# One decode step of attention: PE and DVE in a hand-made order, weights written over the scores, two accumulators, the last output weights behind all of V, two stores

## The chip, the cores and the metric

The kernel runs on one core of one Trainium2 chip. A core has a matrix engine (TensorE, PE in the profile, with its weight loads as PEld), a vector engine (VectorE, DVE), a scalar engine (ScalarE, ACT), GpSimd (POOL) and a queue engine (SyncE, SP), and 16 DMA engines that bring data from the chip's memory (HBM) into the core's own (SBUF). Matrix products land in PSUM, eight banks of 2 KB for each of 128 partitions, from where another engine takes them. The metric is device time in microseconds; before the change the median of three runs is 1333.25.

## What is computed

Everything is float32. Two requests (B = 2), one new token each, attend to a cache of 32768 positions; 32 query heads share 8 key and value heads, 4 to one. Beside it runs a small gated layer on the normalized token.

```python
B, Sq, D = 2, 1, 512
Hq, Hkv, Sk, Dh = 32, 8, 32768, 128

def _A_ref(x, k_cache, v_cache, wq, wo):
    q = (x @ wq).reshape(B, Sq, Hq, Dh).transpose(0, 2, 1, 3)
    k = jnp.repeat(k_cache, rep, axis=1)
    v = jnp.repeat(v_cache, rep, axis=1)
    scores = jnp.einsum("bhqd,bhkd->bhqk", q, k) * (Dh ** -0.5)
    p = _softmax(scores, axis=-1)
    o = jnp.einsum("bhqk,bhkd->bhqd", p, v)
    return o.transpose(0, 2, 1, 3).reshape(B, Sq, Hq * Dh) @ wo

def _B_ref(x, W_gate, W_up, W_down):          # D = 512, F = 1792
    gate = jnp.einsum("bsd,df->bsf", x, W_gate)
    up = jnp.einsum("bsd,df->bsf", x, W_up)
    h = gate * (gate > 0) * up
    return jnp.einsum("bsf,fd->bsd", h, W_down)

xn = _layernorm(x)
return x + _A_ref(xn, k_cache, v_cache, wq, wo) * _silu(_B_ref(xn, W_gate, W_up, W_down))
```

The two caches are 268 MB each and every byte is read once.

## The kernel before

**Tiles.** A group is one request and one key head: 32768 positions, in NU = 8 tiles of TK = 4096 positions, each 2 MB of K and 2 MB of V (16 KB in each of 128 partitions). There are NG = 16 groups and NK = 128 tiles of each kind; `group(g)` takes the two requests of a head one after the other.

**The ring.** All large loads, K, V and the weight matrices, share one pool of SLOTS = 8 slots of 16 KB per partition. All are issued on SP in `load` (line 123), in one order; a load waits on SP until the tile eight loads before it has been read for the last time. The loads run ahead of their use by DEPTH = 3 steps.

**A step.** The main loop (line 448) has one step for each K tile, and V follows K by OFF = 9 steps, since a group's maximum must be known before its weights are. In step `s`:

- `k_transposes(s)`: two VectorE transposes of 128x2048 (line 287) turn the K tile into the layout `kts` that the matrix engine needs.
- `scores(s)`: 16 matmuls (32 instructions in float32, line 298) with the query columns as weights, into a PSUM tile `s`; then VectorE scales them into an SBUF tile `sc` and keeps the running maximum (line 308).
- every eighth step `maximum(g)`: reduce over the group, transpose, reduce, broadcast back as a bias `nb`.
- `weights(v + 1)`: ScalarE takes exp (line 338), a matmul with a permutation spreads the result (`pt`, line 342), VectorE transposes it into one of three buffers `pts` (line 346).
- `values(v)`: 8 matmuls (16 instructions of 128x512, line 355) add weights times V into `o_ps`, one PSUM bank for all groups. The very last V tile is loaded and used in pieces, `LAST = (2, 1, 1)` quarters.
- at a group's end `sums` (the softmax's denominator), `take_o` (line 377: scale `o_ps` into `os`) and `finish_group` (line 386: gather the four query heads from the partitions into `ot`), and after the second request of a head the projection with the output weights `wo` (line 401), added to `yacc` or, for the last head, multiplied by the gate `gy` into `res` (lines 412 and 413).

The order in which PE and DVE issue this is not that of the text: the framework's planner orders the instructions of each engine by its own estimate of what is ready. The loads keep the order of the text. `ahead` holds what is loaded at which step, `extra` the matmuls of the small gated layer; `make_base` prepares `yacc * gy + x` shortly before the end. Output weights of head `hk` are loaded in the step that loads the last V tile of that head.

**The end.** The result lies in 4 x 2 rows of `res` and leaves in four stores, on POOL, SP, ACT and SP:

```python
for c, eng in enumerate((nc.gpsimd, nc.sync, nc.scalar, nc.sync)):
    eng.dma_start(out[:, 0, c * P : (c + 1) * P], res[32 * c : 32 * c + B, :])
```

Of the kernel before, what the change touches and what calls it, by code (L numbers as in the profile page):

```python
# [8 lines left out]
F32 = mybir.dt.float32  # L9
# [11 lines left out]
LAST = (2, 1, 1)  # L21
# [6 lines left out]
def kernel(  # L28
# [31 lines left out]
    spool = ctx.enter_context(tc.tile_pool(name="spool", bufs=NU + LAG + 3))  # L60
    work = ctx.enter_context(tc.tile_pool(name="work", bufs=2))
    ps_s = ctx.enter_context(tc.tile_pool(name="ps_s", bufs=3, space=PSUM))
# [48 lines left out]
    ot = const.tile([P, 2, 2, 32], F32, name="ot")  # L111
    nc.vector.memset(ot, 0.0)
# [5 lines left out]
    o_ps = ps_p.tile([P, NC, DH], F32, name="o_ps", bufs=1)  # L118
    nc.vector.memset(o_ps, 0.0)

    KT, VT, ST, PT, KTS, NBIAS, LS, MX, WO = {}, {}, {}, {}, {}, {}, {}, {}, {}
# [25 lines left out]
    def load_wo(hk):  # L147
        WO[hk] = ring.tile([P, 2, 2, D], F32, tag="r", align_bytes=ALIGN, name=f"wo_{hk}")
        r = REP * DH
        load(  # L150
            WO[hk].rearrange("p c i d -> p c (i d)"),
            wo[hk * r : (hk + 1) * r, :].rearrange("(c p i) d -> p c (i d)", c=2, i=2),
        )
# [78 lines left out]
    def mlp_gu(which):  # L232
        ps = ps_m.tile([P, 512], F32, tag="m", name=f"ps_{which}")
        for k in range(NKC):
            for c in range(4):
# [6 lines left out]
                )  # L242
        sb = work.tile([P, 512], F32, tag="row", name=f"sb_{which}")
        nc.vector.tensor_copy(sb[:, :FC], ps[:, :FC])
# [37 lines left out]
    def k_transposes(t):  # L282
        src = KT.pop(t).rearrange("p c j d -> p (c j d)")
        KTS[t] = ktpool.tile([P, NBLK * DH], F32, tag="kt", name=f"kts_{t}")
        half = NBLK * DH // 2
        for i in range(2):
            nc.vector.transpose(  # L287
                KTS[t][:, i * half : (i + 1) * half], src[:, i * half : (i + 1) * half]
            )

    def scores(t):
        g, u = divmod(t, NU)
        b, hk = group(g)
        ps = ps_s.tile([P, 256], F32, tag="s", name=f"s_{t}")
        mov = KTS.pop(t).rearrange("p (c j e k) -> p e c j k", c=NC, j=NJ, e=4)
        for e in range(4):
            for c in range(4):
# [6 lines left out]
                )  # L304
        if u == 0:
            MX[g] = work.tile([P, NU], F32, tag="mx", name=f"mx_{g}")
        ST[t] = spool.tile([P, 256], F32, tag="s", name=f"sc_{t}")
        nc.vector.tensor_scalar(  # L308
            ST[t], ps, SCALE, None, op0=ALU.mult, op1=ALU.max, accum_out=MX[g][:, u : u + 1]
        )  # L310

    def maximum(g):
        m = work.tile([P, 1], F32, tag="m", name=f"m_{g}")
        nc.vector.reduce_max(m, MX.pop(g), axis=AX.X)
        pr = ps_m.tile([P, 512], F32, tag="m", name=f"pr_{g}")
        nc.tensor.transpose(pr[:1, :P], m, ident)
# [14 lines left out]
        NBIAS[g] = work.tile([P, 1], F32, tag="nb", name=f"nb_{g}")  # L331
        nc.vector.tensor_copy(NBIAS[g], pr[:, 256:257])  # L332
        LS[g] = work.tile([P, NU], F32, tag="ls", name=f"ls_{g}")

    def weights(t):
        g, u = divmod(t, NU)
        st = ST.pop(t)
        nc.scalar.activation(  # L338
            st, st, AF.Exp, bias=NBIAS[g], scale=1.0, accum_out=LS[g][:, u : u + 1]
        )  # L340
        ps = ps_p.tile([P, 256], F32, tag="pt", name=f"pt_{t}")
        nc.tensor.matmul(  # L342
            ps, perm.rearrange("p k c h -> p (k c h)"), st, start=True, stop=True
        )
        PT[t] = work.tile([P, NJ, Q], F32, tag="pt", name=f"pts_{t}", bufs=3)
        nc.vector.transpose(PT[t].rearrange("p j m -> p (j m)"), ps)  # L346

    def values(t):
        g, u = divmod(t, NU)
        v, w = VT.pop(t), PT.pop(t)  # L350
        c = 0
        for n in (NC,) if t < NK - 1 else LAST:
            for j in range(NJ):
                a = Q * (j % 4)
                nc.tensor.matmul(  # L355
                    o_ps[a : a + n * REP, :n, :],
# [10 lines left out]
    def sums(g):  # L367
# [4 lines left out]
        RL[g] = work.tile([P, 1], F32, tag="rl", name=f"rl_{g}")  # L372
        nc.vector.reciprocal(RL[g], pr[:, :1])

    def take_o(g):
        OS[g] = work.tile([P, NC, DH], F32, tag="os", name=f"os_{g}")
        nc.vector.tensor_scalar(OS[g], o_ps, RL.pop(g), None, op0=ALU.mult)  # L377

    def finish_group(g):
        b, hk = group(g)  # L380
# [121 lines left out]
```

## Time and profile before

| | us |
|---|---|
| median of three runs | 1333.25 |
| lowest, highest | 1332.27, 1333.82 |
| the profiled execution | 1335.89 |
| its span | 1334.0 |
| PE busy | 881.1 |
| PE weight loads busy | 345.6 |
| DVE busy | 736.5 |
| ACT busy | 69.1 |
| HBM read | 564.67 MB |

The span is the time from the first to the last instruction in the profile; the profiled execution's own time has 1.89 us more around it. Busy times of different engines overlap. The strip over 40 slices gives the share of each engine in tenths and the rate of the DMA engines in GB/s. In the list of groups a line gives busy time, the mean of one instruction in ns, and the idle time before, with what ended it. In the timeline, a line gives start, length, engine, line of the kernel, operation, what is written from what, and in brackets the idle time before with what ended it. In a table of windows, the columns are the window, its length, the busy time of PE, PEld, DVE, ACT and POOL with their instructions, the granted clock of PE, the share of the DMA engines' time and GB/s.

### The profile page before, as it was taken

What the parts mean: (1) busy time and instruction counts of PE and PEld (TensorE: products, weight loads), DVE (VectorE), ACT (ScalarE), POOL (GpSimd) and SP (SyncE); (2) the same over time, 40 slices, a digit from 0 to 9 for tenths busy, and PEclk for the clock granted to TensorE, in tenths of its full rate; (3) what the DMA queues carried; (4) which work ended last, traced back from release to release, by engine and by line L of the source; (5) the groups of instructions that cost most, each with busy time, mean ns of one, the idle gap of its engine ahead of it and who ended that gap; (6) DMA issues with size and microseconds to landing.
All of it is one profiled execution on the core that took longest, in us unless ns stands there. A gap on an engine that the chain in (4) does not pass through costs nothing.

```text
span 1334.0 us, 17338 instructions
## 1 busy us (share of the span) xinstructions
PE 881.1 (66%) x7560; PEld 345.6 (26%) x7560; DVE 736.5 (55%) x976; ACT 69.1 (5%) x261; POOL 1.3 (0%) x7
## 2 busy tenths in 40 slices
PE   4767566766757666676666757667666766767657
PEld 1333222222213222232222312223222232213213
DVE  5765554555555555564555555465565555556462
ACT  0001010100101001010100101001010100101001
POOL 0000000000000000000000000000000000000000
PEclk9777887988878888788977888888887978878889
DMA  9999999999999999999999999999999999999996
GB/s 397 429 431 429 431 430 430 429 431 431 429 430 431 430 430 430 429 430 432 430 430 422 428 430 431 429 416 429 429 430 430 415 430 429 431 431 414 430 430 283
DMA packets 40907, 565.79 MB, mean 424 GB/s; under 512 B 4462, under 2 KB 4478, under 8 KB 6784
## 3 DMA queue, kind: packets, MB, share of 16 engines
q1 hardware_dynamic: 40776, 564.68, 99.4%
q8 instruction: 60, 0.98, 0.3%
q14 instruction: 15, 0.12, 0.0%
q10 hardware_dynamic: 24, 0.01, 0.0%
q0 software_dynamic: 32, 0.00, 0.0%
HBM read 564.67 MB, written 0.00 MB: 423 GB/s over the span
## 4 chain that ended last, share of the span: by engine, by line
issue 100%; POOLq 0%; POOL 0%
POOLq L497 0%; POOL ident masks.py:199 0%; POOL ident masks.py:197 0%; POOLq masks.py:199 0%; POOLq L484 0%
## 5 line engine op out<-in xcount | busy, mean ns | idle before, releaser
L298 PE MATMUL s<-kts,qt 128*32 128x256 f32 x4096 | 466.7, 522 | 388.9 <-DVE kts L287 373.7
L287 DVE STREAM_TRANSPOSE kts<-k 128x2048 f32<-128x2048 f32 x256 | 572.7, 2275 | 0.0
L355 PE MATMUL o_ps<-v,pts 128*16 128x512 f32 (+2 forms) x2080 | 360.2, 675 | 0.0
L298 PEld LDWEIGHTS s<-kts,qt 128*32 128x32 f32 x4096 | 180.2, 140 | 664.3 <-issue 351.6
L308 DVE TENSOR_SCALAR_CACHE_REDUCE sc<-s 128x256 f32<-128x256 f32 x128 | 54.3, 425 | 375.5 <-PE s L298 375.5
L346 DVE STREAM_TRANSPOSE pts<-pt 128x256 f32<-128x256 f32 x128 | 57.0, 448 | 137.9 <-PE o_ps L355 131.2
L355 PEld LDWEIGHTS o_ps<-v,pts 128*16 128x16 f32 (+2 forms) x2080 | 96.2, 116 | 141.6 <-issue 130.1
L338 ACT ACTIVATE sc<-sc,nb 128x256 f32<-128x256 f32 x128 | 63.2, 494 | 1147.3 <-DVE nb L332 1147.3
L342 PE MATMUL pt<-sc,perm 128*128 128x256 f32 x256 | 85.3, 439 | 33.4 <-DVE pts L346 32.2
L342 PEld LDWEIGHTS pt<-sc,perm 128*128 128x128 f32 x256 | 42.5, 198 | 99.7 <-issue 73.0
L386 PE MATMUL po<-sel,os 128*64 128x4 f32 x512 | 23.4, 204 | 3.9 <-DVE os L377 3.9
L386 PEld LDWEIGHTS po<-sel,os 128*64 128x64 f32 x512 | 22.0, 138 | 10.2 <-DVE os L377 10.2
L338 ACT ACTIVATION_READ_ACCUMULATOR sc<-sc,nb 128x1 f32 x128 | 23.9, 187 | 0.0
L377 DVE TENSOR_SCALAR os<-o_ps,rl 128x512 f32<-128x512 f32 x16 | 12.0, 750 | 17.3 <-PE o_ps L355 17.3
L401 PE MATMUL py<-wo,ot 128*32 128x128 f32 x256 | 19.2, 403 | 0.4 <-DVE ot L396 0.4
L396 DVE COPY ot<-po 64x4 f32<-64x4 f32 x32 | 5.2, 163 | 19.7 <-PE po L386 19.5
L401 PEld LDWEIGHTS py<-wo,ot 128*32 128x32 f32 x256 | 14.1, 153 | 2.5 <-issue 1.5
L192 PE MATMUL pq<-wq,xnt 128*32 128x512 f32 x64 | 10.1, 788 | 1.1 <-DMA wq<-in_A_wq_dram 0.8
L308 DVE DVE_READ_ACCUMULATOR sc<-s 128x1 f32 x128 | 10.7, 83 | 0.0
L180 PE MATMUL px<-ident,boot 32*128 32x32 f32 x4 | 0.9, 288 | 12.8 <-DVE boot L174 12.8
L214 DVE COPY qt<-pqt 32x16 f32<-32x16 f32 x64 | 8.6, 176 | 1.3 <-PE pqt L209 0.9
L332 DVE COPY nb<-pr 128x1 f32<-128x1 f32 x16 | 2.5, 159 | 12.2 <-PE pr L328 12.2
(70 smaller groups left out, 115.3 us busy)
## 6 DMA issues: line engine op xcount, KB each, us to landing
k<-in_A_k_cache_dram SPq DMA_DIRECT2D x128, 2048.0 KB, 18.7
v<-in_A_v_cache_dram SPq DMA_DIRECT2D x127, 2048.0 KB, 17.2
wq<-in_A_wq_dram SPq DMA_DIRECT2D x4, 2048.0 KB, 13.3
wo<-in_A_wo_dram SPq DMA_DIRECT2D x8, 1024.0 KB, 15.5
wg<-in_B_W_gate_dram SPq DMA_DIRECT2D x2, 1792.0 KB
wu<-in_B_W_up_dram SPq DMA_DIRECT2D x2, 1792.0 KB, 33.0
wd<-in_B_W_down_dram SPq DMA_DIRECT2D x2, 1792.0 KB
v<-in_A_v_cache_dram SPq DMA_DIRECT2D x1, 1024.0 KB
```

The lines of the kernel that those rows point to most:

```text
L192: nc.tensor.matmul(pq[half][32 * c : 32 * c + 32, :], xnt[:, k, :], wqt[k][:, half, c * 512 : (c + 1) * 512], start=(k == 0), stop=(k == N ...
L214: nc.vector.tensor_copy(qt[part, b, half * 4 : half * 4 + 4, :, kb * REP + h], src[:, :, :, b],)
L287: nc.vector.transpose(KTS[t][:, i * half : (i + 1) * half], src[:, i * half : (i + 1) * half])
L298: nc.tensor.matmul(ps[Q * c : Q * c + Q, :], qt[:, b, hk, e, :], mov[:, e, c], start=(e == 0), stop=(e == 3),)
L308: nc.vector.tensor_scalar(ST[t], ps, SCALE, None, op0=ALU.mult, op1=ALU.max, accum_out=MX[g][:, u : u + 1])
L338: nc.scalar.activation(st, st, AF.Exp, bias=NBIAS[g], scale=1.0, accum_out=LS[g][:, u : u + 1])
L342: nc.tensor.matmul(ps, perm.rearrange("p k c h -> p (k c h)"), st, start=True, stop=True)
L346: nc.vector.transpose(PT[t].rearrange("p j m -> p (j m)"), ps)
L355: nc.tensor.matmul(o_ps[a : a + n * REP, :n, :], w[:, j, c * REP : (c + n) * REP], v[:, c : c + n, j, :], start=(u == 0 and j < 4), stop=( ...
L377: nc.vector.tensor_scalar(OS[g], o_ps, RL.pop(g), None, op0=ALU.mult)
L386: nc.tensor.matmul(pr[64 * r : 64 * r + 64, i * REP : (i + 1) * REP], o2[:, c, i, :], sel[:, c, :], start=(c == 0), stop=(c == NC - 1),)
L401: nc.tensor.matmul(py[32 * c : 32 * c + 32, :P], ot[:, k // 2, k % 2, :], WO[hk][:, k // 2, k % 2, c * P : (c + 1) * P], start=(k == 0), s ...
```

## The change

**Order.** At the end of each step `pin()` chains the instructions that PE and DVE got in that step, in the order of the text, without a semaphore. The loop's text is rewritten for it: helpers are split into a matrix part and a take by VectorE. In step `s` VectorE has the first half of K's transposes, the taking of the scores of the step before, at a group's start the taking of the finished accumulator, the second half of the transposes, and the taking of the next weights. PE has the next weights, the gathering of a finished group, the scores, the projection, the sums and the values. The loop is one step longer.

**Weights over scores.** `take_weights` transposes the weights from PSUM back into the tile that held the scores (`ST`), and `values` reads them there; the pool has 13 such tiles instead of 12, and the three `pts` buffers go. All exps of a group are issued in `maximum`.

**Two accumulators.** `ops[g % 2]` takes the place of `o_ps`, `ots` holds two of what was `ot`; score tiles in PSUM are two instead of three.

**Output weights.** Those of the last two heads are loaded behind all of V, the last one in two halves; one projection adds both heads in PSUM. `LAST` is `(2, 2)`.

**Stores.** Two, one for each request, on SP and ACT.

```diff
-LAST = (2, 1, 1)
+LAST = (2, 2)
...
-    spool = ctx.enter_context(tc.tile_pool(name="spool", bufs=NU + LAG + 3))
+    spool = ctx.enter_context(tc.tile_pool(name="spool", bufs=NU + LAG + 4))
...
-    ps_s = ctx.enter_context(tc.tile_pool(name="ps_s", bufs=3, space=PSUM))
+    ps_s = ctx.enter_context(tc.tile_pool(name="ps_s", bufs=2, space=PSUM))
...
-    o_ps = ps_p.tile([P, NC, DH], F32, name="o_ps", bufs=1)
-    nc.vector.memset(o_ps, 0.0)
+    ops = [ps_p.tile([P, NC, DH], F32, name=f"o_ps_{i}", bufs=1) for i in range(2)]
+    for i in range(2):
+        nc.vector.memset(ops[i], 0.0)
...
+        if hk < HKV - 1:
+            load(dst, rows)
+        else:
+            for c in range(2):
+                load(dst[:, c], rows[:, c])
...
+    def take_weights(t):
+        nc.vector.transpose(ST[t].rearrange("p j m -> p (j m)"), PW.pop(t))
...
-        v, w = VT.pop(t), PT.pop(t)
+        v, w = VT.pop(t), ST.pop(t)
...
+    def project_o(hks):
+        py = ps_m.tile([P, 512], F32, tag="m", name=f"py_{hks[0]}")
+        for hk in hks:
+            w = WO.pop(hk)
...
     for hk in range(HKV):
-        at(ahead, (hk * B + B) * NU - 1 + OFF - DEPTH, load_wo, hk)
+        end = hk if hk < HKV - 2 else HKV - 1
+        at(ahead, (end * B + B) * NU - 1 + OFF - DEPTH, load_wo, hk)
...
+    def pin():
+        nonlocal pinned
+        for ins in block[pinned:]:
+            e = ins.engine
+            if e not in (mybir.EngineType.PE, mybir.EngineType.DVE):
+                continue
+            if e in last:
+                tc.add_manual_dep(
+                    ins,
+                    last[e].name,
+                    mybir.DependencyInfo(
+                        mybir.DependencyClass.NoSync, mybir.DependencyReason.DATA
+                    ),
+                    reason="order of issue",
+                )
+            last[e] = ins
+        pinned = len(block)
+
-    for s in range(NK + OFF):
+    for s in range(NK + OFF + 1):
         v = s - OFF
+        done = (v - 1) // NU if v > 0 and v % NU == 0 else None
+        live = 0 <= v + 1 < NK
+        first = (v + 1) // NU if live and (v + 1) % NU == 0 else None
         if s < NK:
-            k_transposes(s)
+            k_transpose(s, 0)
+        if 0 < s <= NK:
+            take_scores(s - 1)
+        if done is not None:
+            take_o(done)
+        for f, a in taken.get(s, []):
+            f(*a)
+        if first is not None:
+            tile_maximum(first)
+        elif live:
+            weights(v + 1)
+        if s < NK:
+            k_transpose(s, 1)
+        if first is not None:
+            maximum(first)
+        elif live:
+            take_weights(v + 1)
+        if done is not None:
+            finish_group(done)
+        if s < NK:
             scores(s)
...
+            if g % B == B - 1 and hk != HKV - 2:
+                project_o((hk,) if hk < HKV - 1 else (hk - 1, hk))
+        if first is not None:
             weights(v + 1)
+            take_weights(v + 1)
+        if 0 <= v < NK:
             if v % NU == NU - 1:
                 sums(v // NU)
             values(v)
...
+        pin()
...
-    for c, eng in enumerate((nc.gpsimd, nc.sync, nc.scalar, nc.sync)):
-        eng.dma_start(out[:, 0, c * P : (c + 1) * P], res[32 * c : 32 * c + B, :])
+    rows = res.rearrange("(c q) n -> q c n", q=32)
+    for b, eng in enumerate((nc.sync, nc.scalar)):
+        eng.dma_start(out[b, 0, :].rearrange("(c n) -> c n", c=4), rows[b])
```

138 lines of the change are left out of this document (76 added, 62 removed).

## The prediction

> **What bounds the kernel now.** I read the page's rates first, then the same rates cut into stages, then the waits of VectorE, the time from issue to landing of loads early and late, and last the timeline of the end.
>
> From the page:
>
> ```profile
> span 1334.0 us, 17338 instructions
> DVE  5765554555555555564555555465565555556462
> DMA  9999999999999999999999999999999999999996
> GB/s 397 429 431 429 431 430 430 429 431 431 429 430 431 430 430 430 429 430 432 430 430 422 428 430 431 429 416 429 429 430 430 415 430 429 431 431 414 430 430 283
> q1 hardware_dynamic: 40776, 564.68, 99.4%
> ```
>
> The loads run at 429 to 432 GB/s nearly throughout; VectorE (DVE) is busy about half of each slice. But four of the late slices dip to 414 to 422, and the last holds 283. The dips by stage (columns: window, length, busy of each engine, granted clock, DMA share, GB/s):
>
> ```profile
> 10.00:720.00 710.00, 469.30 (x3950) 184.26 (x3950) 399.85 (x555) 35.48 (x132) 0.00 (x0) 0.83 1.01 430
> 720.00:740.00 20.00, 13.04 (x130) 4.68 (x130) 12.55 (x11) 0.00 (x0) 0.00 (x0) 0.91 1.00 414
> ...
> 880.00:900.00 20.00, 12.61 (x130) 4.68 (x130) 12.75 (x10) 0.00 (x0) 0.00 (x0) 0.91 0.99 404
> ...
> 1040.00:1060.00 20.00, 12.18 (x127) 4.58 (x130) 13.18 (x10) 0.00 (x0) 0.00 (x0) 0.91 1.00 405
> ...
> 1200.00:1220.00 20.00, 11.76 (x120) 4.34 (x124) 13.61 (x10) 0.00 (x0) 0.00 (x0) 0.91 0.99 403
> ```
>
> Against 430 these four lose (16 + 26 + 25 + 27) x 20 / 430 = 4.4 us. Why there, and only late? Time from issue to landing, one line from each of four stages (issues at 240 to 320 us, at 1200 to 1280 us, the one K at 1209.3, and the kernel's very first load):
>
> ```profile
> k<-in_A_k_cache_dram SPq DMA_DIRECT2D x8, 2048.0 KB, 20.8
> ...
> k<-in_A_k_cache_dram SPq DMA_DIRECT2D x7, 2048.0 KB, 15.4
> ...
> k<-in_A_k_cache_dram SPq DMA_DIRECT2D x1, 2048.0 KB, 10.4
> ...
> wq<-in_A_wq_dram SPq DMA_DIRECT2D x1, 2048.0 KB, 7.7
> ```
>
> A load meets a backlog of 21 us early and of 15 us late: the queue is eaten up slowly, because slots of the ring come back a little more slowly than the loads could use them. At 1209.3 it is nearly empty (10.4, against 7.7 for a load that met nothing). So two chains run almost level: the loads, and the work that frees slots. That work's step:
>
> ```profile
> 1268.16 4.46 DVE L287 STREAM_TRANSPOSE kts<-k 128x2048 f32<-128x2048 f32 x2
> ...
> 1276.28 0.42 DVE L308 TENSOR_SCALAR_CACHE_REDUCE sc<-s 128x256 f32<-128x256 f32 x1 [3.65 <-PE s L298]
> ...
> 1278.00 0.45 DVE L346 STREAM_TRANSPOSE pts<-pt 128x256 f32<-128x256 f32 x1 [1.28 <-PE o_ps L355]
> ```
>
> 4.46 us of transposes, 3.65 waiting for the scores, 0.5 to take them, 1.28 waiting for the values, 0.45: 10.2 us with the seams. A K and a V tile are 4.19 MB, 9.75 us at 430 GB/s. Over the run:
>
> ```profile
> DVE sc L308 <- PE s L298: 375.5, 126, 3.7
> DVE pts L346 <- PE o_ps L355: 131.2, 79, 2.7
> ...
> DVE st L167 <- DMA boot<-in_A_x_dram: 2.9, 1, 2.9
> ```
>
> The end is the other place (timeline, then the landing of the load issued at 1310.17):
>
> ```profile
> 1310.17 0.38 SPq L123 DMA_DIRECT2D wo<-in_A_wo_dram  x1
> ...
> 1314.55 1.91 PE L355 MATMUL o_ps<-v,pts 128*16 128x512 f32 x16
> ...
> 1317.72 8.80 PE L355 MATMUL o_ps<-v,pts 128*16 128x512 f32 x112
> ...
> 1326.59 0.75 DVE L377 TENSOR_SCALAR os<-o_ps,rl 128x512 f32<-128x512 f32 x1 [4.72 <-PE o_ps L355]
> ...
> 1327.40 1.46 PE L386 MATMUL po<-sel,os 128*64 128x4 f32 x32 [0.87 <-DVE os L377]
> 1328.89 0.34 DVE L396 COPY ot<-po 64x4 f32<-64x4 f32 x2 [1.55 <-PE po L386]
> ...
> 1329.29 1.08 PE L401 MATMUL py<-wo,ot 128*32 128x128 f32 x32 [0.43 <-DVE ot L396]
> 1330.44 0.29 DVE L412 TENSOR_TENSOR res<-py,gy 128x128 f32<-128x128 f32 x1 [1.20 <-PE py L401]
> ...
> 1331.08 0.65 SPq L470 DMA_DIRECT2D out_dram<-res  x2
> ...
> 1331.35 0.65 POOL L470 DMA_DIRECT2D out_dram<-res  x1 [1330.04 <-DVE res L413]
> ```
>
> ```profile
> wo<-in_A_wo_dram SPq DMA_DIRECT2D x1, 1024.0 KB, 15.5
> ```
>
> The last load lands at 1310.17 + 15.5 = 1325.7; the last values end at 1326.5 and 7.5 us follow. How the loads end:
>
> ```profile
> 1322.00:1323.00 1.00, 1.00 (x16) 0.35 (x12) 0.00 (x0) 0.00 (x0) 0.00 (x0) 1.00 0.51 197
> ...
> 1324.00:1325.00 1.00, 1.00 (x16) 0.33 (x12) 0.00 (x0) 0.00 (x0) 0.00 (x0) 1.00 0.22 90
> ```
>
> Half the DMA engines have run out by 1322; the others work until about 1325. A tile has landed when its slowest engine is done, so the late half sets the end, and a pause of the early half in a dip costs nothing in itself.
>
> **The change, part by part. The hand-made order.** In a step VectorE now does: first half of the transposes, the previous tile's scores, second half, the next weights. The 3.65 us wait is covered by the weights and the next first half (0.45 + 2.2), the 1.28 goes because the transposed weights overwrite their own scores instead of waiting for one of three buffers. That leaves 4.46 + 0.5 + 0.45 = 5.4 us of VectorE in a step, against 9.75 of loads. What is late next is the landing of K: the transposes wait for it, and scores, weights and values are queued behind them. A V tile's slot then comes back some 13 us after it landed: 4.9 until its K is there, 5.4, and 2 to 4 for scores and values. V tiles reuse a slot four steps (39 us) on, so its next load still goes out about 25 us ahead: the queue does not run dry. TensorE (PE), should it run at half clock:
>
> ```profile
> 1282.88 3.20 PE L298 MATMUL s<-kts,qt 128*32 128x256 f32 x26 [1.48 <-DVE kts L287]
> ...
> 1291.40 1.70 PE L298 MATMUL s<-kts,qt 128*32 128x256 f32 x26 [1.48 <-DVE kts L287]
> ```
>
> The same 26 instructions take 1.88 times as long there: the 32 of the scores 3.9, the values (1.91 for a tile's 16, above) 3.6, the weights, two of the same width as the scores, 0.25 and their latency: about 8, still under 9.75.
>
> So the dips should go. What that is worth is bounded by 0 (all of them fell on the early engines) and by 4.4 us (all 16 alike). The K at 1209.3 took 10.4 us in the emptiest stretch against 7.7 without a backlog, so the late engines still had work there; the value is near the lower end. I take **-1.0**.
>
> **The end.** The output weights of head 6 (1.05 MB) go from 1199 to behind all of V, so two megabytes follow the last V instead of one. With the loads' end kept at 1325.7, V's last half lands 2.10 MB, 4.9 us, earlier: 1320.8. It needs 16 instructions of 128x256, 1.70 / 26 x 16 = 1.05: 1321.85. From the values' end (1317.72 + 8.80 = 1326.52) to the projection at 1329.29 are 2.77 us, unchanged: 1324.6. The projection now does two heads, 64 instructions, 2 x 1.08 = 2.16: 1326.8. It reaches the last half of the weights after 48 of them, at 1326.2, when that has landed. From its end (1330.37) to the store's issue at 1331.08: 0.71. From there the old end is 2.92 us away; the last of the four stores leaves POOL at 1332.0, the last of the two would leave SP about 1331.4, so 2.3. Sum: 1326.8 + 0.7 + 2.3 = 1329.8 against 1334.0: **-4.2**. That the compute arrives in time for this rests on the step above: TensorE has then nothing left over when V's last half lands, where now the last 112 instructions run without a pause from 1317.72.
>
> **At nothing:** clearing a second accumulator and a second ot, some tenths of a microsecond of VectorE ahead of the layernorm, where it waits 2.9 us for x (without that cover, nothing of it would reach the loads either, which have a backlog). The split of the last weights: one more issue of about 0.4 us on SP, which is waiting for slots. The softmax terms moved between queues, and the mlp's copies one step later: inside the 4 us per step that VectorE has free. Two score banks instead of three: the scores before last are long taken.
>
> **Against which time.** The profiled execution took 1335.89 (span 1334.0), 2.64 above the median 1333.25. Where those 2.64 sit no row shows. If in the compute at the end, which now lags V's landing, runs without a profile have that much less to win; bounds 0 and 2.6, and since the loads fill most of the span alike I take +0.8. Sum for the median: -4.2 - 1.0 + 0.8 = -4.4: **1328.9**, say 1329.
>
> **The rivals. Cold TensorE at the end.** Now TensorE waits for each V. The trace has this:
>
> ```profile
> 1279.43:1282.84 3.41, 0.62 (x4) 0.17 (x4) 3.40 (x2) 0.00 (x0) 0.00 (x0) 1.00 0.99 423
> 1282.84:1286.25 3.41, 3.37 (x30) 1.52 (x34) 0.00 (x0) 0.00 (x0) 0.00 (x0) 0.50 1.03 442
> ...
> 1296.49:1299.90 3.41, 1.93 (x33) 0.91 (x30) 1.73 (x1) 0.00 (x0) 0.00 (x0) 1.00 0.97 411
> ```
>
> A window of 3.41 us with 0.62 us of matmul is followed by one at half clock; one with 1.93 was not. At the end a V comes each 4.9 us with 1.91 + 0.25, about 2.2 us of matmul, so a window holds 0.8 to 2.2, and which it is depends on phase. Price if cold from V's last half on: values +0.9, po up to +1.3, projection +1.9, together 2 to 4, I take 3. Then -1.4: about 1332, no change. Against it: from V's next-to-last tile to the projection's end, 1.9 + 1.05 + 1.05 + 1.46 + 2.16 = 7.6 us of matmul fall into about 11.5 us (1315 to 1326.8), 2.2 per window. The Trainium skill ("TensorE: Matmul & The Clock Gate", Part 1: The HAM clock gate) says that TensorE falls to half rate after a whole idle window of about 3.4 us; the gaps of some 2.6 us here would by that leave it at full rate and the sum as it is. The rows above show it stricter: 0.62 us of work in a window did not save it, which is why this rival has a chance of 0.25.
>
> **All 16 engines lose in the dips.** Then the 4.4 us come back whole: -4.2 - 4.4 + 0.8 = -7.8, about 1325.4. For it: the share falls below 1.00. Against: 10.4 at 1209.3.
>
> **Slots come back later than now.** With VectorE's order fixed, everything of a step stands behind K's landing, and at a group's first step also behind the maximum, the scores and the first weights. Now a head of two groups takes 878.21 - 717.78 = 160.4 us, a group of 8 steps 80.2:
>
> ```profile
> 717.78 0.38 SPq L123 DMA_DIRECT2D wo<-in_A_wo_dram  x1
> ...
> 878.21 0.38 SPq L123 DMA_DIRECT2D wo<-in_A_wo_dram  x1
> ```
>
> If a group took longer than that, every microsecond over would cost 16, one per group: at 81, +13 us, 1346. My working gives 8 x 5.4 to 8 and, for that first step, an allowance of one more step: 49 to 72. It decides only above 80.2.
>
> **How the numbers follow.** The forecast has 0.50, all engines lose 0.13: faster, 0.63. The cold end, or a full 2.6 of the profile's surplus, 0.26: within 0.2% (2.7 us, about what a measurement of this kernel can tell from no change). Slots later: 0.11. The range goes from the second rival's end (1324.8) to the first's cold end with 4 us (1332.8); it leaves out the slow case and little more. The forecast's own: 1327 to 1330.5.
>
> **What the profile would show.** Right: no slice under 425 GB/s before the last; VectorE's wait for the scores down from 375 to under 60 us and idle time ahead of the transposes that ends with K's landing; times from issue to landing of 23 us or more also late; V's last half landed some 5 us before the last weights; TensorE at full clock in the last 10 us. Wrong: a dip that stays (something else than empty slots), a loads' end earlier than 1323 (the dips did cost all engines) or later than 1326, half clock after 1320, or a projection that waits for wo.

## The result

In the comparison of the two kernels on one chip the changed kernel takes 1330.95 us (median of 20 runs, 1330.04 to 1333.91), the kernel before 1333.67 (20 runs, 1332.27 to 1336.53). The ratio is 0.9981, 95% interval 0.9975 to 0.9987: a gain of 0.19%, about 2.5 us (the medians lie 2.7 apart), where the forecast had 4.4. It lies in the forecast's range, and just on the line of 0.2% between the case that was given 0.63 and the one that was given 0.26.

The profiled execution after the change takes 1330.78 us, its span is 1328.9: 5.1 us less than the profiled execution before, where the forecast had 5.2 ahead of its last term. So the two profiles agree with the sum, and the medians do not. The page after:

```profile
span 1328.9 us, 17052 instructions
DVE  5775555555645555554555555545555554646541
DMA  9999999999999999999999999999999999999996
GB/s 397 430 430 431 430 429 431 430 430 430 430 431 429 431 431 430 429 430 431 429 431 428 431 431 430 431 429 431 431 428 431 429 431 431 429 431 430 431 431 288
```

No slice but the first and the last is under 428 GB/s. Two of the stretches that dipped to 414 and 403, from a table of windows with the columns of before, and then VectorE's waits (us in total, times, longest) and the time from issue to landing of K tiles issued from 1200 to 1280 us:

```profile
720.00:740.00 20.00, 12.26 (x95) 4.75 (x99) 9.50 (x18) 4.04 (x16) 0.00 (x0) 0.74 1.00 426
...
1200.00:1220.00 20.00, 12.95 (x101) 5.11 (x101) 10.81 (x20) 4.04 (x16) 0.00 (x0) 0.83 1.01 431
```

```profile
DVE kts L298 <- DMA k<-in_A_k_cache_dram: 459.6, 114, 6.0
...
DVE sc L374 <- PE pt L365: 82.3, 22, 5.2
...
DVE sc L322 <- PE s L308: 5.5, 6, 1.7
```

```profile
k<-in_A_k_cache_dram SPq DMA_DIRECT2D x5, 2048.0 KB, 27.0
```

VectorE waited 375.5 us for scores and 131.2 for the values; now it waits 459.6 for K to land, and 82.3 for the spread weights, most of it in the first step of a group. A K load issued from 1200 to 1280 us lands 27.0 us later instead of 15.4. The end, in the timeline:

```profile
1314.88 3.37 PE L383 MATMUL o_ps<-v,sc 128*16 128x512 f32 x16 [1.03 <-DMA v<-in_A_v_cache_dram]
...
1318.49 2.20 PE L383 MATMUL o_ps<-v,sc 128*8 128x256 f32 x32
...
1319.64 0.55 PEld L383 LDWEIGHTS o_ps<-v,sc 128*8 128x8 f32 x16 [0.60 <-DMA v<-in_A_v_cache_dram]
1320.76 0.75 DVE L406 TENSOR_SCALAR os<-o_ps,rl 128x512 f32<-128x512 f32 x1 [1.99 <-PE o_ps L383]
...
1321.56 1.46 PE L416 MATMUL po<-sel,os 128*64 128x4 f32 x32 [0.87 <-DVE os L406]
...
1322.95 2.25 PE L434 MATMUL py<-wo,ots 128*32 128x128 f32 x64
...
1324.56 0.38 PEld L434 LDWEIGHTS py<-wo,ots 128*32 128x32 f32 x16 [0.35 <-DMA wo<-in_A_wo_dram]
...
1325.60 0.29 DVE L445 TENSOR_TENSOR res<-res,base 128x128 f32<-128x128 f32 x1
1325.91 0.65 SPq L551 DMA_DIRECT2D out_dram<-res  x1
1325.92 0.61 ACTq L551 DMA_DIRECT2D out_dram<-res  x1
```

V's last half has landed by 1319.6, the projection waits 0.35 us for the last half of the weights, which are there at 1324.6, and the stores leave at 1325.91, 5.2 us before those of the profiled execution before. From there to the end of the span it is 3.0 us, as before (2.92).

### The profile page after: what moved, and what is told of

Read it like the earlier page. It is cut to its first block, busy times and chain, and to the rows that moved or that the text cites. A ratio compares the mean times of both kernels' runs of the same rounds, so it can differ in the third digit from the quotient of the medians.

```text
span 1328.9 us, 17052 instructions
## 1 busy us (share of the span) xinstructions
PE 872.7 (66%) x7544; PEld 338.5 (25%) x7544; DVE 727.7 (55%) x976; ACT 69.1 (5%) x261; POOL 0.7 (0%) x6
## 4 chain that ended last, share of the span: by engine, by line
DMA 74%; DVE 14%; PE 11%; issue 0%; DVEq 0%
DMA k<-in_A_k_cache_dram 68%; DVE kts L298 12%; PE s L308 5%; PE o_ps L383 4%; DMA v<-in_A_v_cache_dram 2%; DMA wo<-in_A_wo_dram 2%; DMA wq<-in_A_wq_dram 2%; DVE sc L322 1%; PE pt L365 0%; DVE qt L220 0%; PE ps_u L242 0%; PE ps_d L281 0%; DVE os L406 0%; PE pq L198 0%; DVE boot L212 0%
## 5 line engine op out<-in xcount | busy, mean ns | idle before, releaser
L298 DVE STREAM_TRANSPOSE kts<-k 128x2048 f32<-128x2048 f32 x256 | 590.4, 2307 | 459.6 <-DMA k<-in_A_k_cache_dram 459.6
L308 PE MATMUL s<-kts,qt 128*32 128x256 f32 x4096 | 455.1, 526 | 326.5 <-DVE kts L298 322.5
L383 PE MATMUL o_ps<-v,sc 128*16 128x512 f32 (+1 forms) x2064 | 343.0, 685 | 6.2 <-DMA v<-in_A_v_cache_dram 6.1
L383 PEld LDWEIGHTS o_ps<-v,sc 128*16 128x16 f32 (+1 forms) x2064 | 91.4, 115 | 149.6 <-issue 136.4
L374 DVE STREAM_TRANSPOSE sc<-pt 128x256 f32<-128x256 f32 x128 | 53.1, 415 | 82.4 <-PE pt L365 82.3
L365 PE MATMUL pt<-sc,perm 128*128 128x256 f32 x256 | 94.5, 453 | 0.9 <-ACT sc L359 0.9
L351 PE MATMUL pr<-negone,mrow 1*128 1x1 f32 x32 | 8.9, 344 | 37.5 <-DVE mrow L348 37.5
L351 PEld LDWEIGHTS pr<-negone,mrow 1*128 1x128 f32 x32 | 7.5, 291 | 40.8 <-DVE mrow L348 40.8
L434 PE MATMUL py<-wo,ots 128*32 128x128 f32 x256 | 12.6, 313 | 0.1
L434 PEld LDWEIGHTS py<-wo,ots 128*32 128x32 f32 x256 | 10.5, 131 | 2.0 <-issue 0.9
```

What stands on the lines that cost most here:

```text
L298: nc.vector.transpose(KTS[t][:, i * half : (i + 1) * half], src[:, i * half : (i + 1) * half])
L308: nc.tensor.matmul(ps[Q * c : Q * c + Q, :], qt[:, b, hk, e, :], mov[:, e, c], start=(e == 0), stop=(e == 3),)
L351: nc.tensor.matmul(pr[:, 256:257], mrow.rearrange("o c k h -> o (c k h)"), negone, start=True, stop=True)
L365: nc.tensor.matmul(PW[t], perm.rearrange("p k c h -> p (k c h)"), ST[t].rearrange("p j m -> p (j m)"), start=True, stop=True,)
L374: nc.vector.transpose(ST[t].rearrange("p j m -> p (j m)"), PW.pop(t))
L383: nc.tensor.matmul(ops[g % 2][a : a + n * REP, :n, :], w[:, j, c * REP : (c + n) * REP], v[:, c : c + n, j, :], start=(u == 0 and j < 4), ...
```

## The experiments

Ratios are to runs of the kernel before on the same chip, with 95% intervals; they are taken over all runs and can differ a little from the ratio of two medians. Where nothing else is said, a kernel computes all that the changed one does.

**The kernel before, once more.** No edit.

> The kernel before, unchanged, for the profile of a second execution. Theory (the profiled execution of before was a late one: its compute at the end lagged behind V's landing by some 3 us, and the term I set at 0.8 us for that was too small): an execution near the median has a span of 1331 to 1332, its last values end within 1 to 2 us of V's landing instead of 3.2, and the last load lands at 1325 to 1326 as in the first profile. Rival (what differs is the whole loop or the transfers): the last load lands 2 us or more earlier, and everything behind it is shifted alike.

Measured: 1332.72 us (10 runs, 1332.34 to 1336.63), ratio 0.9997 (0.9986 to 1.0007); the span of its profiled execution is 1331.0, 3.0 less than that of the first. An early load and the last one, in the queue's timeline of the first profiled execution and of this one:

```profile
236.50 0.39 SPq L123 DMA_DIRECT2D wo<-in_A_wo_dram  x1
...
1310.17 0.38 SPq L123 DMA_DIRECT2D wo<-in_A_wo_dram  x1
```

```profile
233.22 0.39 SPq L123 DMA_DIRECT2D wo<-in_A_wo_dram  x1
...
1306.88 0.38 SPq L123 DMA_DIRECT2D wo<-in_A_wo_dram  x1
```

Both lie 3.3 us apart, and so does every tenth load between them, to 0.03 us; the difference comes up between 70 and 155 us and then stays to the end. The last load nevertheless lands within 0.4 us of the same time in both. So the loads do not set the pace of the issues; the work that frees the slots does, and a late start of that chain is never made up.

The earlier chain also leaves this execution only two dips, where the first had four. Two of the stretches, and the end:

```profile
880.00:900.00 20.00, 14.80 (x145) 5.17 (x137) 11.09 (x18) 0.45 (x2) 0.00 (x0) 0.91 1.01 431
1040.00:1060.00 20.00, 14.55 (x142) 5.36 (x145) 11.28 (x19) 0.02 (x1) 0.00 (x0) 0.91 0.99 404
```

```profile
1314.43 9.04 PE L355 MATMUL o_ps<-v,pts 128*16 128x512 f32 x112
...
1326.23 1.08 PE L401 MATMUL py<-wo,ot 128*32 128x128 f32 x32 [0.43 <-DVE ot L396]
...
1328.02 0.65 SPq L470 DMA_DIRECT2D out_dram<-res  x2
```

The last values end at 1323.5 instead of 1326.5, though the last weights land at nearly the same time in both, 1325.3 and 1325.7. This is what the theory said. Most of the kernel's runs lie near this execution, and the 1335.89 of the first belongs to the late ones (here two of ten, 1336.4 and 1336.6; in the comparison above five of 20, from 1335.6 up).

**The order alone.** The changed kernel with the old end.

```diff
-LAST = (2, 2)
+LAST = (2, 1, 1)
-        end = hk if hk < HKV - 2 else HKV - 1
-        at(ahead, (end * B + B) * NU - 1 + OFF - DEPTH, load_wo, hk)
+        at(ahead, (hk * B + B) * NU - 1 + OFF - DEPTH, load_wo, hk)
-            if g % B == B - 1 and hk != HKV - 2:
-                project_o((hk,) if hk < HKV - 1 else (hk - 1, hk))
+            if g % B == B - 1:
+                project_o((hk,))
```

The last weights come in one load and the four old stores are back.

> The changed kernel with the end as before: output weights of head 6 at their old place, one projection per head, LAST = (2, 1, 1), the last weights whole, four stores. Left: the hand-made order, weights over scores, two accumulators. Theory (the dips cost only the DMA engines that are ahead; the order is worth 1 us in the loads' end and what the compute no longer lags): no dips, loads end at 1324 to 1325, a span some 1 to 1.5 us above the changed kernel's 1328.9 (V's last half lands 2.4 later, projection 1.1 shorter, store 0.6 longer), 1332 to 1332.7 by the median. Rival (the order brings the whole gain): equal to the changed kernel, 1331. Rival (the order is worth nothing): equal to before, 1333.7.

Measured: 1332.25 us (11 runs), ratio 0.9987 (0.9978 to 0.9996), no dip, store at 1327.58, as the theory had it. Order, buffers and accumulators together are worth 1.2 us by the medians and 1.7 by the ratio.

**The end alone.** The kernel before with the change's end.

```diff
-LAST = (2, 1, 1)
+LAST = (2, 2)
-    ot = const.tile([P, 2, 2, 32], F32, name="ot")
+    ots = const.tile([P, 2, 2, 2, 32], F32, name="ots")
...
-        at(ahead, (hk * B + B) * NU - 1 + OFF - DEPTH, load_wo, hk)
+        end = hk if hk < HKV - 2 else HKV - 1
+        at(ahead, (end * B + B) * NU - 1 + OFF - DEPTH, load_wo, hk)
```

The last weights in two halves, the projection of two heads and the two stores are as in the change.

> The kernel before with the end of the changed one: output weights of heads 6 and 7 behind all of V, the last in halves, one projection for both, LAST = (2, 2), two stores; order, buffers and accumulator as before. Theory (in before the compute at the end is late by itself, so V's earlier landing can't be used, and the projection is longer): dips as before, the last values end no earlier than 1325, time within 1 us of before, 1333 to 1334.5. Rival (the end alone brings the gain): 1331.

Measured: 1336.32 us (12 runs, 1331.32 to 1339.97), ratio 1.0013 (1.0001 to 1.0025), above the 1333 to 1334.5 that was expected. The values and the store of the profiled execution (1338.90):

```profile
1320.40 8.79 PE L358 MATMUL o_ps<-v,pts 128*16 128x512 f32 x96
...
1334.11 0.64 SPq L477 DMA_DIRECT2D out_dram<-res  x1
```

The last weights land at 1325.1, but the values lag to 1329.2: loads that come in a better order are worth nothing where the work behind them is late. Three of the four dips stay (422, 400 and 407 GB/s). Two of the twelve runs took 1331.3 and 1331.9, about as long as the changed kernel; that these are the ones with an early chain would fit, but only their times are known.

**No fixed order.** The changed kernel without `pin()`, so that the planner orders PE and DVE.

```diff
-        pin()
```

> The changed kernel without the chain of instructions: PE and DVE in the planner's order, all else as changed. Theory (any order that keeps a step under 9.75 us does): if the planner's order keeps VectorE's wait for the scores under 200 us in sum, 1331 to 1331.5 and no dips. Rival (the written order is what frees the slots): VectorE waits for scores 350 us or more again, dips come back in the second half, and the time is 1332.5 to 1334.

Measured: 1330.73 us (7 runs), ratio 0.9973 (0.9963 to 0.9984), no dip. VectorE's waits:

```profile
DVE sc L322 <- PE s L308: 352.3, 125, 3.7
DVE kts L298 <- DMA k<-in_A_k_cache_dram: 102.6, 63, 3.8
```

The 3.7 us wait for the scores is back at nearly every tile and costs nothing. Neither case came as it was written: the theory had asked for a wait under 200 us, and the rival for dips at 350. The hand-made order is not needed to remove the dips.

**Nine buffers.** The kernel before, with one number changed.

```diff
-        PT[t] = work.tile([P, NJ, Q], F32, tag="pt", name=f"pts_{t}", bufs=3)
+        PT[t] = work.tile([P, NJ, Q], F32, tag="pt", name=f"pts_{t}", bufs=9)
```

> The kernel before with nine buffers pts instead of three, nothing else. Theory (what kept the slots back was VectorE's 1.28 us wait in each step for a free pts buffer, that is, for the values of three tiles ago; without it a step takes 8.9 us, less than the 9.75 of its loads): the 131 us of that wait fall below 30, VectorE begins to wait for K's landing, issue to landing stays above 20 us to the end, no slice before the last is under 425 GB/s, and the time is that of the order alone, 1332.0 to 1332.7. Rival (the serial wait for the scores keeps the slots back, and only the written order helps): dips as before, 1333 to 1334.

Measured: 1331.97 us (12 runs, 1331.78 to 1332.14), ratio 0.9986 (0.9977 to 0.9994): as much as the order alone, and all runs within 0.4 us where those of before spread over 4.

```profile
DVE sc L308 <- PE s L298: 350.5, 126, 3.7
...
DVE kts L287 <- DMA k<-in_A_k_cache_dram: 112.4, 67, 3.5
...
DVE pts L346 <- PE pt L342: 26.4, 54, 2.0
```

```profile
1200.00:1220.00 20.00, 15.96 (x149) 7.92 (x153) 11.30 (x25) 4.04 (x16) 0.00 (x0) 0.83 1.01 429
```

```profile
k<-in_A_k_cache_dram SPq DMA_DIRECT2D x5, 2048.0 KB, 29.8
```

The wait of `pts` for `o_ps`, 131.2 us in 79 waits, is gone, the wait for the scores is not, the dips are, and 29.8 us pass from issue to landing late in the run. In the kernel before, taking away the wait for a buffer is enough to bring the slots back in time.

**Order, but three buffers and one accumulator.** The changed kernel, pinned, with `o_ps` for all groups and three `pts` buffers as before.

```diff
-        nc.vector.transpose(ST[t].rearrange("p j m -> p (j m)"), PW.pop(t))
+        PT[t] = work.tile([P, NJ, Q], F32, tag="pt", name=f"pts_{t}", bufs=3)
+        nc.vector.transpose(PT[t].rearrange("p j m -> p (j m)"), PW.pop(t))
...
-                    ops[g % 2][a : a + n * REP, :n, :],
+                    o_ps[a : a + n * REP, :n, :],
```

> The changed kernel with one accumulator and with three separate pts buffers in place of the weights written over the scores; order chained as changed. Theory (in the written order the buffer of three tiles ago is long free, and the accumulator is taken before the next group's first values are issued): no dips, no wait of VectorE for a pts buffer above 20 us in sum, 1331 as the changed kernel. Rival (the second accumulator or the in-place weights are what freed the slots): dips return or a group's first step grows by 2 us or more, and the time goes to 1332 to 1334.

Measured: 1330.63 us (10 runs), ratio 0.9978 (0.9969 to 0.9987), no dip, 451.1 us of waiting for K. In the written order the second accumulator and the weights in place are worth nothing.

**Three buffers and no order.** The changed kernel without `pin()`, with three `pts` buffers and the two accumulators.

```diff
-        nc.vector.transpose(ST[t].rearrange("p j m -> p (j m)"), PW.pop(t))
+        PT[t] = work.tile([P, NJ, Q], F32, tag="pt", name=f"pts_{t}", bufs=3)
+        nc.vector.transpose(PT[t].rearrange("p j m -> p (j m)"), PW.pop(t))
...
-        pin()
```

> The changed kernel in the planner's order (no chain) and with three separate pts buffers: the counterpart of the nine buffers in the kernel before. Theory (the buffers, not the order, decide): VectorE waits again for values ahead of the weights, 100 us or more in sum, dips come back in the second half or issue to landing falls below 18 us, and the time is 1331.5 to 1333.5, above the 1330.7 of the planner's order with the weights in place. Rival: 1330.7 and no dips, since the rest of the change is enough.

Measured: 1349.42 us (4 runs), ratio 1.0114 (1.0091 to 1.0137). The wait is back, the queue nearly empty from 1200 to 1280:

```profile
DVE pts L376 <- PE o_ps L385: 135.8, 79, 4.1
```

```profile
k<-in_A_k_cache_dram SPq DMA_DIRECT2D x8, 2048.0 KB, 9.6
```

With the changed kernel, the one without a fixed order and the one with three buffers in order this makes a square: either the order or the buffers will do, and without both the slots come back late. That this is slower even than before was not expected. Against "the end alone" its K transposes fall some 3.3 us behind between 430 and 530 us and as much again between 910 and 1010, and keep step within a microsecond elsewhere from 150 us on; what happens there stays open.

**Which DMA engines are late.** The changed kernel with small loads of 8, 4, 2 and 1 partitions behind the last weights, which nobody reads; their packets show when single engines come free.

```diff
+    def load_probe():
+        for i, (n, e) in enumerate(((8, 192), (4, 320), (2, 384), (1, 448))):
+            load(probe[:n, i, :e], wq[:n, :e])
+    at(ahead, NK - 1 + OFF - DEPTH, load_probe)
```

> The changed kernel with four very small loads (8, 4, 2 and 1 rows of wq, of sizes that nothing else has) issued behind the last weights into a tile that nobody reads; it adds four issues on SP and 8 KB. It asks which DMA engines are the late ones. If a load of n rows goes to n engines in a fixed order, the small packets start where those engines have finished their queue. Theory (the lag of 11.8 us at the end is one of single engines, always the same): the packets of the 8-row load start in two clumps, about 1313 and 1321 to 1325, and those of 4, 2 and 1 rows tell on which side the first engines are. Rival (the lag is one of the transfers, not of engines): all start within 2 us of each other. The time is within 1 us of the changed kernel.

Measured, packet starts: the load of 8 partitions at 1312.71, 1312.76, 1312.84, 1313.96, 1314.72, 1319.58, 1322.29 and 1323.53; the load of 4 at 1312.75, 1312.80, 1314.00 and 1319.62; those of 2 and of 1 within 0.9 us of their issue. The lag belongs to single engines: some are done 11 us before others. This execution (one run, 1332.99 us, 2.0 over the changed kernel where at most 1 was expected) also had a TensorE at half clock at the end: `po` took 2.38 us instead of 1.46 and `py` 3.64 instead of 2.25.

**Four stores without POOL.** The changed kernel with four stores of two rows.

```diff
-    rows = res.rearrange("(c q) n -> q c n", q=32)
-    for b, eng in enumerate((nc.sync, nc.scalar)):
-        eng.dma_start(out[b, 0, :].rearrange("(c n) -> c n", c=4), rows[b])
+    for c, eng in enumerate((nc.sync, nc.scalar, nc.sync, nc.scalar)):
+        eng.dma_start(out[:, 0, c * P : (c + 1) * P], res[32 * c : 32 * c + B, :])
```

> The changed kernel with the four stores of 2 x 128 of before, issued on SP, ACT, SP and ACT (none on POOL), in place of the two stores of 4 x 128. From the end of res to the end of the span it was 2.95 us with POOL's store among the four, and 3.0 us with the two. Theory (a store that gathers four partitions costs its queue 0.65 us of issue where one of two partitions costs 0.33 or 0.26, and its packets leave 1.26 to 1.54 us after res, against 0.77): 2.4 to 2.7 us, so 0.3 to 0.6 less, about 1330.5 where the changed kernel has 1330.95. Rival (the receipt of the last store takes what it takes, whoever issues): 3.0 us still.

Measured: 1330.48 us (11 runs), ratio 0.9976 (0.9967 to 0.9985).

```profile
1326.00 0.29 DVE L445 TENSOR_TENSOR res<-res,base 128x128 f32<-128x128 f32 x1
1326.32 0.65 SPq L550 DMA_DIRECT2D out_dram<-res  x2
1326.33 0.56 ACTq L550 DMA_DIRECT2D out_dram<-res  x2
```

From the end of `res`, 1326.29, to the end of the span, 1329.0, it is 2.7 us, against 3.0: at the upper edge of what the theory allowed. The two medians differ in the same direction (1330.95), but the intervals overlap: a gain over the changed kernel is not shown by the times.

**The least that does it.** The kernel "the end alone" with nine `pts` buffers and the four stores; planner's order, one accumulator.

```diff
-        PT[t] = work.tile([P, NJ, Q], F32, tag="pt", name=f"pts_{t}", bufs=3)
+        PT[t] = work.tile([P, NJ, Q], F32, tag="pt", name=f"pts_{t}", bufs=9)
...
+    for c, eng in enumerate((nc.sync, nc.scalar, nc.sync, nc.scalar)):
+        eng.dma_start(out[:, 0, c * P : (c + 1) * P], res[32 * c : 32 * c + B, :])
```

> The kernel before with 9 pts buffers in place of 3, with the change's end (both last output weights behind all of V, one projection for two heads, LAST (2, 2)) and the four stores on SP, ACT, SP and ACT; the planner's order, one accumulator, weights in their own buffers. Theory (all that counted in the change is that slots come back in time, and the end): as the changed kernel with the same stores, 1330.2 to 1331, no dip, last V landed some 5 us before the last weights. Rival (in the end, the fixed order is needed: with the end alone and 3 buffers, the last values ended at 1329.2, 4 us after the loads): 1332 to 1336.

Measured: 1330.60 us (11 runs, 1330.15 to 1333.37), ratio 0.9979 (0.9970 to 0.9988): not to be told from the changed kernel. There is no dip (428 to 432 GB/s in the four stretches). Its profiled execution (span 1331.6) is one with a cold end. The values of the last tiles, and then windows in which the last columns are granted clock, DMA share and GB/s:

```profile
1314.78 1.91 PE L358 MATMUL o_ps<-v,pts 128*16 128x512 f32 x16 [1.54 <-DMA v<-in_A_v_cache_dram]
...
1317.21 1.05 PE L358 MATMUL o_ps<-v,pts 128*8 128x256 f32 x16 [0.52 <-DMA v<-in_A_v_cache_dram]
...
1319.55 1.78 PE L358 MATMUL o_ps<-v,pts 128*8 128x256 f32 x16 [1.29 <-DMA v<-in_A_v_cache_dram]
...
1322.18 2.38 PE L389 MATMUL po<-sel,os 128*64 128x4 f32 x32 [0.85 <-DVE os L380]
...
1324.49 3.64 PE L406 MATMUL py<-wo,ots 128*32 128x128 f32 x64
```

```profile
1318.00:1319.00 1.00, 0.26 (x8) 0.00 (x0) 0.00 (x0) 0.00 (x0) 0.00 (x0) 1.00 0.58 233
...
1320.00:1321.00 1.00, 1.00 (x16) 0.18 (x4) 0.00 (x0) 0.00 (x0) 0.00 (x0) 0.50 0.51 209
```

**Bytes moved to the early engines, twice.** The kernel with four stores, and a few partitions of two V tiles in small loads that only the first four or two DMA engines carry.

```diff
+        n = {118: 4, 122: 2}.get(t)
+        if n:
...
+            m = P - 8 * n
+            load(flat[:m], rows[:m])
+            for i in range(8):
+                load(flat[m + i * n : m + (i + 1) * n], rows[m + i * n : m + (i + 1) * n])
```

> The same stores, and 32 partitions of V tile 118 loaded by 8 loads of 4 partitions, and 16 partitions of V tile 122 by 8 loads of 2, so that these bytes are carried by 4 and by 2 DMA engines, the ones that the probe found ahead of the others (of the four, three are some 11 us ahead and one some 5; both of the two are ahead). Theory (loads end with the slowest DMA engines, which are 10 to 11.8 us behind the early ones): each late engine has 1.2 + 0.6 = 1.8 us less to carry, the loads end 1.5 to 1.9 us earlier (about 1322.8), the last V too, and the time falls by 1 to 1.8 us against the four stores alone, to about 1329.2. Rival (the lag is not of fixed engines, or moves with the program): the chosen engines become the last ones, the loads end later, and the time rises by 0 to 4 us. Rival (the rate as a whole sets the end): no difference.

Measured: 1355.34 us (5 runs), ratio 1.0158 (1.0144 to 1.0172), 25 us slower. The nine loads of tile 118 went out like this:

```profile
1240.45 37.39 SPq L126 DMA_DIRECT2D v<-in_A_v_cache_dram  x9
```

Each of the later ones waited 4 to 10 us for the landing of the load eight before it. That is not the whole loss: from about 1254 to 1278, while the tile's load of 96 partitions is carried, a packet of 16 KB takes 1.0 to 1.3 us (means over 5 us) instead of 0.61. The second try goes by the waits alone and has four small loads for a tile instead of eight:

```diff
+        if t in (108, 116):
...
+            load(flat[:112], rows[:112])
+            for i in range(112, P, 4):
+                load(flat[i : i + 4], rows[i : i + 4])
```

> The four stores on SP, ACT, SP and ACT, and the last 16 partitions of V tiles 108 and 116 in four loads of 4 partitions each (carried by 4 DMA engines), the other 112 partitions in one load on all 16. Loads take turns on eight semaphores, and a load waits until the one eight before it on the same semaphore has landed, which made the loads of 4 and 2 partitions of the former try wait 5 to 10 us each and let the queue run empty; here the four small ones of a tile leave four large ones in flight, 19.5 us of loads, more than the lag of 11 us, so the queue should not run dry. Theory (loads end with the slowest DMA engines): each late engine carries 0.6 us less for each of the two tiles, the four early ones 1.8 us more each, which their lead covers; the loads end 1.0 to 1.3 us earlier, the median 0.8 to 1.3 us under that of the four stores alone (1330.48): about 1329.4. Rival (the semaphores hold the queue up here too): a slice under 425 GB/s near 1140 or 1220 us and a time at or above 1330.5. Rival (the lag follows the rate as a whole or other engines): loads' end unchanged, 1330.5.

Measured: 1357.16 us (5 runs), ratio 1.0175 (1.0161 to 1.0189). Windows around tile 108:

```profile
1145.00:1155.00 10.00, 8.93 (x89) 3.48 (x92) 6.56 (x9) 0.00 (x0) 0.00 (x0) 0.83 1.02 433
1155.00:1165.00 10.00, 5.31 (x40) 1.71 (x36) 5.19 (x5) 0.00 (x0) 0.00 (x0) 0.71 1.04 257
1165.00:1175.00 10.00, 3.72 (x30) 1.08 (x22) 0.00 (x0) 0.00 (x0) 0.00 (x0) 0.84 0.98 220
1175.00:1187.00 12.00, 5.93 (x46) 2.14 (x48) 5.19 (x5) 0.00 (x0) 0.00 (x0) 0.52 1.00 248
```

The engines are busy all the time (share 0.98 to 1.04) and move little more than half: it is not an empty queue, which was the rival's reason for the lost time. A packet of 16 KB takes 0.61 us until 1156 and 1.0 to 1.3 us (means over 4 us) from then to 1184. Whether balanced engines would end the loads earlier stays open; both tries lost far more than there was to win.

## Why the prediction was right and where it was not

**The dips, -1.0: right.** They are gone, loads meet the 27 us backlog that was forecast (25), and the last load lands at 1324.6 instead of 1325.7 (1325.3 in the second execution of before): 0.7 to 1.1 us, not 4.4. The rival in which all 16 engines lose is out. The landings show where the dips went: in the kernel before, the 16 parts of one load land within 6.1 us at 707 us, within 4.0 at 906, behind two dips, and within 3.9 for the last load, while without dips the spread goes on growing (below). The dips used up the lead of the early engines.

**Why they went: half right.** The step that failed says that the order covers the 3.65 us wait and the buffers the 1.28, and sums both to 5.4 us. The waits went as it says, but taking one of them away is enough: without the shorter one a step is 4.46 + 3.65 + 0.5 + 0.45 = 9.1 us, without the longer one 4.46 + 0.5 + 1.28 + 0.45 = 6.7, both under the 9.75 of the loads. The prediction had every number for this and did not take the two waits one at a time. Nine buffers in the kernel before do the whole of it. Its working also covers 3.65 us with 0.45 + 2.2 = 2.65, which by its own numbers leaves 1.0; measured are 5.5 us of that wait in all, as VectorE now stands behind K's landing.

**The end.** V's last half was forecast for 1320.8, 1319.8 with the dips, and is there at 1319.6. The projection was forecast for 1324.6, 1323.6 with the dips, and starts at 1322.95; it reaches the last half of the weights 0.35 us before that has landed, so that a sign of being wrong, a projection that waits for `wo`, came up in a small size. The store was forecast at 1326.8 + 0.7, less 1.0 for the dips, 1326.5, and leaves at 1325.91. One term failed: **two stores -0.6** measured 0. A store that collects four separate partitions holds its queue for 0.65 and 0.61 us, one of two adjacent rows for 0.25 to 0.33 (two with the pause between them in 0.65 and 0.56), so that two such stores cost what four did. "The last of the two would leave SP about 1331.4" took the duration of the old stores for the new shape. That the first profile agrees with the sum to 0.1 us is luck: the store is 0.6 us earlier than forecast, and what follows it 0.7 longer.

By the runs, the end's own edits are worth about a microsecond and not 4.2: with the order 1332.25 becomes 1330.95, with nine buffers 1331.97 becomes 1330.60 (with four stores), and by the ratios it is 0.8 and 0.9. Most of the 4.2 was the lag of one execution's compute. Its last values ended at 1326.52, 3.3 us after V's last piece had landed; those of the second execution of before ended at 1323.47, 0.7 us after. Against the span of that execution, 1331.0, the 1329.8 of the working is -1.2.

**The profile's surplus, +0.8: mis-sized, and this is what the forecast lost.** The prediction bounded it by 0 and 2.64 and took a low value, "since the loads fill most of the span alike". The repeated profile shows the whole difference in the compute: its span is 3.0 us shorter, its store 3.06 us earlier, its loads' end only 0.4. Against that execution the change gains 2.1 us in the span, against the median of 20 runs 2.7. With +2.6, the upper bound, in place of +0.8 the sum would have been 1330.7. Where slots set the pace, a late execution stays late, and its surplus goes when slots set it no longer; that the twelve runs with nine buffers lie within 0.4 us fits this. The prediction gave the cold end 0.25 and the cold end or the full surplus together 0.26, so that the full surplus, which is what came, had 0.01 by itself. The low end of its range, 1324.8, comes out of no sum that it shows.

**The rivals.** The cold clock came up in the changed kernel's profile, but it was over in time. Windows of 1 us; the third column from the end is the granted clock:

```profile
1316.00:1317.00 1.00, 1.00 (x8) 0.19 (x4) 0.00 (x0) 0.00 (x0) 0.00 (x0) 0.50 0.62 262
...
1318.00:1319.00 1.00, 1.00 (x18) 0.60 (x18) 0.17 (x1) 0.00 (x0) 0.00 (x0) 1.00 0.59 246
```

That is why the values at 1314.88 took 3.37 us instead of 1.91, and it cost nothing: with full clock there, in the kernel with four stores, the last values end at the same time. At the very end the cold clock came up in the kernel with the small loads and in "the least that does it", and cost 0.92 us for `po` and 1.39 for `py`, 2.3 together, where 2 to 4 had been taken. In the kernel with four stores it came later, at 1324.2, and cost about 0.4:

```profile
1322.91 2.70 PE L434 MATMUL py<-wo,ots 128*32 128x128 f32 x64
```

Two of the changed kernel's 20 runs, 1333.40 and 1333.91, would fit such an end, but only their times are known. The Trainium skill ("TensorE: Matmul & The Clock Gate", Part 1: The HAM clock gate) asks for a whole idle window of some 3.4 us before the rate is halved; the rows of "the least that does it" disagree, since there no pause between matmuls from 1310 to 1320 is longer than 1.54 us and the clock is 0.50 at 1320. Slots that come back later are out: 27.0 us from issue to landing.

## What to carry to other kernels

Where two chains run almost level, take the waits of the slower one away one at a time on paper, shortest means first: here one number for a buffer did what a rewritten order, a second accumulator and weights in place did. Profile the kernel before twice: an offset of the issues that stays constant while the loads end together says that the loads do not set the pace, and the times say how far the first profile stands from the median. Shortening the end by moving loads paid here only once the work behind the loads kept up; alone it cost 0.13%.

## What was not expected of the hardware

**The DMA engines drift apart.** One load's landing is spread over 16 engines, and in the changed kernel the spread grows: 0.9 us for the first load, 3.4 at 320 us, 9.0 at 950 us, 11.8 for the last one. When each engine had done its part of the last load, in us:

```
1312.7 1312.8 1312.9 1313.1 1313.2 1314.2 1314.5 1319.6
1322.3 1322.8 1322.9 1322.9 1322.9 1323.0 1324.4 1324.5
```

The last engine falls back in jumps of 1.3 to 1.5 us. A queue that brings the program's instructions moves 59 packets of 16 KB, 0.88 to 1.16 us long, one every 13 to 30 us from 100 us on. Between one load and the next, from 110 to 1320 us, the lags of the 16 engines behind the first grow in sum by 1.05 us where such a packet lies between (54 cases) and by 0.14 where none does (199). So the jumps go with these packets in time; that they are the cause is not shown, as no run was made to change their number.

**Loads of other than 128 partitions.** In the last kernel packets got slower when the first engines began the load of 112 partitions and recovered at 1186 to 1187, when the last had done it; in the first try it was the same with the load of 96. The Trainium skill ("DMA: Bandwidth & Descriptors", The descriptor swizzle) says that in a load to 128 partitions each engine writes one port of SBUF; that shares of seven partitions break this, and that engines then wait for each other, would fit the rows, but no run has such a load without the small ones beside it.
